# A fused attention and gated-MLP kernel: two moves put on another queue, two sums put ahead of the additions, one transpose group a slot sooner

## The chip, the core and the metric

The kernel runs on one core of one Trainium2 chip. Its time is device microseconds of that core, from start to end of the program. The engines are named as the profile names them: PE (TensorE's matrix products; PEld is its loading of weights), DVE (VectorE), ACT (ScalarE), POOL (GpSimd) and SP (SyncE, which only issues DMAs here). "ACTq" and "SPq" are rows of an engine's sequencer, mostly DMA issues. A line number such as L844 is a line of the kernel before.

## The reference

Eight batches of eight heads attend to keys and values that are averaged over groups of 8 positions; the result, turned into 4608 tokens of 512, goes through two large products with a function between them. All of it is float32.

```python
def _attn_ref(q, k, v):                     # each (8, 8, 576, 64)
    k_p = k.reshape(B, H, 72, 8, D).mean(axis=3)
    v_p = v.reshape(B, H, 72, 8, D).mean(axis=3)
    scores = 1.0 / np.sqrt(D) * np.matmul(q, k_p.transpose(0, 1, 3, 2))
    scores = scores - np.max(scores, axis=-1, keepdims=True)
    attn = np.exp(scores)
    attn = attn / (np.sum(attn, axis=-1, keepdims=True) + 1e-09)
    return np.matmul(attn, v_p)

def _moe_ref(x, w_in, w_out, alpha):        # (4608, 512), (512, 2048), (2048, 512), (2048,)
    h = x @ w_in
    s = np.sin(alpha * h)
    g = h + s * s / (alpha + 1e-09)
    return g @ w_out
```

## The kernel before, in words

**Stages.** A short beginning computes most of batch 0's attention. Then come nine units of 512 tokens each (`hidden`), which compute h, the sine and g and store g to a buffer in DRAM (`g_bridge`). The last stage (`outputs`) reads g back and multiplies by w_out. While unit u computes, it also carries the attention of batch u+1: the functions `exp`, `norm`, `turn`, `move`, `all_values` and so on are called in its slots.

**Slots of a unit.** The product x @ w_in is done by a scheme with seven block products instead of eight. A unit has four groups, J = 0 to 3, of 256 columns of w_in for each half; each group has seven slots, k = 0 to 6, one block product (`product`, L844: four matmuls of 128x128 by 128x256, which the profile shows as eight rows) to a slot. So a unit has 28 slots, and slot 21 is the first of group 3. The products of a group come in the order 1, 5, 6, 2, 7, 3, 4. They accumulate in four PSUM banks, and a group takes four of five banks in turn, so that the first bank of the next group is the one that held `b7` of the group before. Between them ACT copies one bank into the next (`copy`, L820: b6 from b1 in slot k=1, b7 from b6 and p5 from b5 in k=3), takes sines (`sin`, L994) and squares (`square`, L1001), and DVE makes sums (`add`, L819). A product that goes on in a copied bank must wait for the copy.

A group G is not done when its slots are. In k=0 of the next group come its last four sines (`last_sines`), in k=1 its last squares, and in k=2 `finish` adds (L1046, two additions, the first of which reads the old `b7`). In k=3 `store_g` (L1060) sends two DMAs of 512 KB to `g_bridge` from SP. The old group is called Q there. One tile `s` holds the sines of all groups.

**Extras.** `carry(u)` fills a table: slot number to functions. `at(15, A.norm, 2)` puts the call into slot 15. In most slots the extras come ahead of that slot's product; in k=2 they come right after `finish(Q)`, in k=0 after `last_sines(Q)`, in k=1 after the copy and the squares. Every engine runs its instructions in the order in which the program gives them out; nothing else orders them but the waits for data. So a call's slot sets its place in the queues of all engines that it uses.

**Attention of batch 1 in unit 0.** `A` is batch 1 and `A0` batch 0. Its scores are shifted by their maxima into a tile `ex`. `exp(i)` (L366, ACT) works on quarter i in place; switching ACT between sine and exponential shows as ACT_TABLE_LOAD. `norm(i)` sums the exponentials (L372, DVE), inverts the sum (L373, DVE) and multiplies (L374, POOL). `turn(i)` transposes the quarter in blocks of 32x32 on DVE into a tile `tr` (L501 to L511). `move(blocks, queue, halves)` (L514) then copies `tr`, block by block, to the tile `aM`, whose partitions are keys: two DMAs (L521) for each block and half, 32 rows of 736 or 704 columns each, on the given queue, SP if none is given. Half 0 is rows 0 to 63 of `aM`, half 1 rows 64 to 127. Each of the four blocks of `tr` is needed for all 32 rows of a quarter's four turns, so no move can start before the last turn. In slot 26 `all_values` (L600) multiplies `aM` with the averaged values (L610, L623). Its first two matmuls read rows 64 to 127 of all four blocks; the next read rows 0 to 63 also.

**Last weights of batch 0.** The last 64 queries of batch 0 go their own way: `norm_rest` (L450) leaves their weights in the tile `last`, `a_rest` (L487) turns them with five transposes on PE (L491, L492) and copies the result to `last_t` on ACT (L493), and `values_rest` (L587) multiplies it with values (L593, L595) in slot 24. Its four parts write four PSUM banks, the last of them the bank that `finish` has freed.

**What follows on the same queues.** `turn_q` (L215) transposes the queries of batch 2 into the same tile `tr` on DVE (L228 and L233, slots 23 and 24), which has to wait for all moves out of `tr`, and moves them with 16 DMAs on SP (L243, slots 25 and 26). The scores of batch 2 (`two_scores`, L317) read them in slots 3 and 5 of unit 1, after eight and after all of the 16.

**Semaphores of DMAs.** All DMAs of SP and ACT together take eight completion semaphores in turn, in the program's order. A DMA's issue waits for the landing of the last one that had its semaphore, so the 16 moves also wait, each, for one about eight DMAs earlier.

Of the kernel before, what the change touches and what calls it, by code (L numbers as in the profile page):

```python
# [40 lines left out]
class Kernel:  # L41
# [1127 lines left out]
    def carry(self, u):  # L1169

        nc = self.nc
        x = defaultdict(list)
        at = lambda slot, f, *a: x[slot].append(lambda: f(*a))
        last = self.B - 1
        b = u + 1
        if u == 0:
            A0, A = self.att[:2]
            at(1, A0.rest_q)
            at(1, A0.a_head, 1, (5, 6, 2))
            at(1, self.refine)  # L1180
            at(2, A0.values, (2, 3), (2, 1), 1, 1)
            at(2, A0.score, 4)
            at(2, self.sums_of_x, 0, 2)
            at(2, self.sums_of_x, 0, 3)
            at(2, self.load_w_in_part, 2)
            at(2, self.load_w_in_part, 3)
            at(2, self.pairs_q, 1, (0, 1))
            at(3, self.pairs_q, 1, (2, 3, 4))
            at(4, self.combine_w_in, 1, (0, 1, 2, 3), self.nc.gpsimd)
            at(4, A.q_t, 0, self.nc.vector.tensor_copy)  # L1190
            at(4, A.q_t, 1, self.nc.vector.tensor_copy)
            at(4, A.k_t)
            at(7, self.load_v, 1)
            at(7, lambda: self.pool_v())
            for i in range(2):
                at((6, 11)[i], A.two_scores, i)
            at(13, A.two_shifts)
            for i in range(2, 5):
                at((8, 8, 9)[i - 2], A.q_t, i)
            at(9, A0.exp, 4)  # L1200
            for i in range(4):
                at((9, 9, 15, 15)[i], A.exp, i)
                at((10, 10, 16, 16)[i], A.norm, i)
                at((13, 13, 19, 19)[i], A.turn, i)
            at(8, self.combine_w_in, 2, (0, 1, 2, 3), self.nc.gpsimd)
            at(13, A0.norm_rest)
            at(17, self.combine_w_in, 3, (0, 1), self.nc.gpsimd)
            at(17, self.combine_w_in, 3, (2, 3), self.nc.gpsimd)
            at(22, A0.a_rest)
            at(24, lambda: A0.values_rest((5, 6, 7, (self.turn + 1) % 5)))  # L1210
            for r in (32, 96):
                at(3, self.nc.gpsimd.memset, self.aM[r:r + 32, :, 704:736], 0.0)
            at(19, A.move, range(3))
            at(20, A.move, (3,), nc.scalar, (0,))
            at(21, A.move, (3,), nc.scalar, (1,))
            at(26, A.all_values)
            at(9, self.load_q, 2)
            at(23, self.inner_w_in)
            for e in range(2):
                at(12, self.load_k, 2, e)  # L1220
                at(17, lambda e=e: self.pool_k[e]())
            at(27, self.att[2].k_t)
            turn = 23
        else:
            at(0, self.sums_of_x, u, 2)
            at(0, self.sums_of_x, u, 3)
        if 0 < u < last:
            A = self.att[b]
            for i in range(2):
                at((3, 5)[i], A.two_scores, i)  # L1230
            at(6, A.two_shifts)
            for i in range(4):
                at((8, 9, 10, 10)[i], A.exp, i)
                at((9, 10, 11, 12)[i], A.norm, i)
                at((12, 13, 13, 13)[i], A.turn, i)
            at(14, A.move, range(4))
            at(6, self.load_v, b)
            at(12, lambda: self.pool_v())
            for i in range(2):
                if b < last:  # L1240
                    at(12, self.load_k, b + 1, i)
                    at(12, lambda i=i: self.pool_k[i]())
            at(25, A.all_values)
            if b < last:
                at(26, self.att[b + 1].k_t)
            if 2 < u + 2 <= last:
                at(7, self.load_q, u + 2)
            at(2, self.inner_x, u)
            turn = 22
        elif u:  # L1250
            turn = None
        if turn and u + 2 <= last:
            for part in range(4):
                at(((turn, turn + 1) if u == 0 else (23, 24))[part] if part < 2 else turn + part, self.turn_q, u + 2, part)
        if u + 1 < self.NU:
            at(27, self.sums_of_x, u + 1, 0)
            at(27, self.sums_of_x, u + 1, 1)
        return x
# [336 lines left out]
```

## Time and profile before

| what | value |
|---|---|
| time, median of 3 runs | 905.26 us (904.72 to 905.44) |
| the profiled execution's own time | 904.95 us |
| its span, first to last instruction | 903.2 us |
| granted TensorE clock | 1.000 of full speed |
| PE busy | 895.0 us (99%) |
| DVE, ACT, POOL busy | 681.0 (75%), 449.1 (50%), 212.6 us (24%) |
| PE busy from 20 to 57 us | 36.90 of 37.00 us |
| PE busy from 357 to 412 us (a later unit) | 55.00 of 55.00 us |
| last stage, 467 to 903.2 us, PE busy | 431.63 of 436.20 us |

How to read it: times in the timeline are microseconds from the start of the span. A row gives start, duration, engine, line, operation, output tile <- input tiles, shapes, and a count where several are merged. In square brackets stands the idle time of that engine just before the row and, behind the arrow, what ended it. Where a wait is for several things, the last one by the profile is named. In the stretches the columns are PE, PEld, DVE, ACT and POOL busy time with their counts, then the granted clock, the DMA engines' share and GB/s. The chain is the sequence of work that ended last, followed backwards. Matmuls are pipelined, and their ends are modelled; two rows of one slot overlap, so the distance between starts tells more than the durations.

Unit 0 begins at about 20 us. Its slot 20 begins at 65.93, slot 22's product at 70.04, slot 23's at 72.55, and slot 26 (`all_values`) at 79.52. Unit 1 begins at about 87 us.

### The profile page before, as it was taken

Reading aid. Unit: us, or ns where it says so; the run is one execution under the profiler, and the core shown is the slowest. Engines: PE = TensorE matmul, PEld = TensorE weight load, DVE = VectorE, ACT = ScalarE, POOL = GpSimd, SP = SyncE. Lnnn points to the kernel's source line nnn. Section 1 sums busy time; section 2 is a strip of 40 time slices with the busy share of each in tenths; the row PEclk is TensorE's granted clock in tenths of the full one; section 3 lists DMA queues with packets and bytes.
Section 4 is the critical chain, followed back from the end, with each engine's and each line's share of the span. In section 5 each row is a group of like instructions: output and inputs, shape, how many; then the busy total and the mean of one; then the engine's idle time right before and its main releaser. Section 6 shows DMA issues by size and latency. Waiting matters only on the chain.

```text
span 903.2 us, 17920 instructions
## 1 busy us (share of the span) xinstructions
PE 895.0 (99%) x7002; PEld 815.1 (90%) x7002; DVE 681.0 (75%) x1012; ACT 449.1 (50%) x1072; POOL 212.6 (24%) x216
## 2 busy tenths in 40 slices
PE   8999999999999999999999999999999999999998
PEld 5787888888888888888888999999999999999998
DVE  7685766768577685764557799979798888889895
ACT  5686776877768778687976611111111111111111
POOL 5688552824438253430000000000000000000000
PEclk9999999999999999999999999999999999999999
DMA  9965867759577595648217246261618162533401
GB/s 253 255 200 151 219 166 196 194 149 270 145 212 186 174 238 138 180 141 298 93 67 232 98 139 205 53 198 40 224 27 227 37 192 72 171 92 123 141 14 40
DMA packets 128746, 141.12 MB, mean 156 GB/s; under 512 B 46920, under 2 KB 95704, under 8 KB 128664
## 3 DMA queue, kind: packets, MB, share of 16 engines
q1 hardware_dynamic: 125880, 137.88, 53.5%
q10 hardware_dynamic: 2784, 2.11, 0.9%
q8 instruction: 55, 0.90, 0.4%
q14 instruction: 27, 0.22, 0.1%
HBM read 75.37 MB, written 47.19 MB: 136 GB/s over the span
## 4 chain that ended last, share of the span: by engine, by line
PE 95%; DVE 2%; ACT 2%; DMA 1%; POOL 0%; SPq 0%; ACTq 0%; issue 0%; DVEq 0%
PE PS L844 44%; PE PS L1328 41%; PE PS L1024 3%; PE PS L317 2%; PE PS L610 2%; PE PS L623 1%; DMA home<-in_k_dram 1%; DVE x L1283 1%; ACT s L1001 0%; DVE s L1283 0%; DVE r L1283 0%; ACT s L994 0%; PE PS L568 0%; PE PS L289 0%; PE PS L278 0%; PE PS L566 0%
## 5 line engine op out<-in xcount | busy, mean ns | idle before, releaser
L844 PE MATMUL PS<-home,a 128*128 128x256 f32 x1104 | 258.0, 381 | 0.4 <-DVE h L819 0.2
L844 PEld LDWEIGHTS PS<-home,a 128*128 128x128 f32 x1104 | 205.2, 190 | 33.3 <-issue 5.0
L844 PE MATMUL PS<-home,as 128*128 128x256 f32 x768 | 182.9, 382 | 0.5 <-ACT PS L820 0.5
L844 PEld LDWEIGHTS PS<-home,as 128*128 128x128 f32 x768 | 141.6, 190 | 20.6 <-ACT PS L820 1.2
L1378 POOL TENSOR_TENSOR cc<-cc,cb 128x576 f32<-128x576 f32 x1 | 2.0, 1980 | 501.8 <-DVE cb L1283 501.8
L1328 PE MATMUL PS<-s,wb 128*128 128x144 f32 x896 | 119.1, 286 | 0.0
L1328 PEld LDWEIGHTS PS<-s,wb 128*128 128x128 f32 x896 | 113.7, 190 | 0.1
L1001 ACT ACTIVATE s<-s,c 128x256 f32<-128x256 f32 (+1 forms) x228 | 113.5, 564 | 0.0
L819 DVE TENSOR_TENSOR h<-PS,p 128x512 f32<-128x512 f32 x72 | 49.2, 683 | 62.0 <-PE PS L844 36.9
L131 POOL TENSOR_TENSOR kvin<-kvin 96x768 f32<-96x768 f32 (+3 forms) x42 | 72.7, 1731 | 71.7 <-DMA kvin<-in_v_dram 69.3
L1456 ACT COPY PS<-PS 128x144 f32<-128x144 f32 x56 | 14.7, 263 | 144.8 <-PE PS L1328 138.1
L994 ACT ACTIVATE s<-h,al 128x256 f32<-128x256 f32 x144 | 65.6, 509 | 38.3 <-DVE h L819 38.1
L1328 PE MATMUL PS<-r,wb 128*128 128x144 f32 x512 | 73.3, 286 | 0.3 <-DVE r L1283 0.3
L1328 PE MATMUL PS<-s,a 128*128 128x144 f32 x512 | 73.2, 286 | 0.0
L994 ACT ACTIVATE s<-PS,al 128x256 f32<-128x256 f32 x144 | 60.2, 470 | 20.2 <-PE PS L844 19.2
L1046 DVE TENSOR_TENSOR h<-PS,s 128x512 f32<-128x512 f32 x36 | 24.7, 685 | 58.6 <-ACT s L1001 58.6
L1328 PEld LDWEIGHTS PS<-r,wb 128*128 128x128 f32 x512 | 67.1, 190 | 0.5 <-DVE r L1283 0.5
L1328 PEld LDWEIGHTS PS<-s,a 128*128 128x128 f32 x512 | 67.0, 190 | 0.0
L820 ACT COPY PS<-PS 128x512 f32<-128x512 f32 x72 | 41.5, 576 | 34.9 <-PE PS L844 30.1
L1476 ACT COPY PS<-PS 128x144 f32<-128x144 f32 x56 | 14.7, 263 | 88.1 <-PE PS L1328 88.1
L1046 DVE TENSOR_TENSOR h<-h,s 128x1024 f32<-128x1024 f32 x36 | 57.1, 1586 | 0.9 <-ACT s L1001 0.9
L1328 PE MATMUL PS<-x,wb 128*128 128x144 f32 x384 | 54.9, 286 | 0.0
(216 smaller groups left out, 1409.6 us busy)
## 6 DMA issues: line engine op xcount, KB each, us to landing
g_bridge<-h SPq DMA_DIRECT2D x72, 512.0 KB
r<-g_bridge SPq DMA_DIRECT2D x31, 1152.0 KB
out_dram<-o SPq DMA_DIRECT2D x122, 72.0 KB
kvin<-in_k_dram SPq DMA_DIRECT2D x14, 576.0 KB
q<-in_q_dram SPq DMA_DIRECT2D x7, 1024.0 KB
kvin<-in_v_dram SPq DMA_DIRECT2D x14, 512.0 KB
aM<-tr SPq DMA_DIRECT2D x54, 92.0 KB
aM<-tr SPq DMA_DIRECT2D x54, 88.0 KB
```

Source lines behind the costliest of these rows:

```text
L131: self.nc.gpsimd.tensor_tensor(out=t[..., 0:w] if w > D else out, in0=t[..., 0:w], in1=t[..., w:2 * w], op=OP.add)
L317: nc.tensor.matmul(ps[e][r0 + r:r0 + r + q.shape[-1], h, :], q[s], kb[s, hp, :], start=True, stop=True)
L610: nc.tensor.matmul(o[r:r + 64], w, x, start=start and i < 2, stop=False, skip_group_check=True)
L819: add = lambda o, x, y: nc.vector.tensor_tensor(out=o, in0=x, in1=y, op=OP.add)
L820: copy = lambda o, x: nc.scalar.copy(out=o, in_=x)
L844: nc.tensor.matmul(ps[:, jj, :], self.A[p][:, kk, f * P:(f + 1) * P], x[:, kk, :], start=(start and n == 0), stop=(kk == 1), skip_group_ch ...
L994: self.nc.scalar.activation(out=G.s[:, i, jj, j, :], in_=src[:, jj], func=AF.Sin, scale=self.al[:, f:f + 1])
L1001: self.nc.scalar.activation(out=x, in_=x, func=AF.Square, scale=self.c[:, f:f + 1])
L1024: nc.tensor.matmul(o, W[m][:, G.J - J0], X[m], start=start and n == 0, stop=True, skip_group_check=True)
L1046: add = lambda o, x, y: self.nc.vector.tensor_tensor(out=o, in0=x, in1=y, op=OP.add)
L1328: nc.tensor.matmul(out, W[:, J // 2, J % 2, :], A[:, J, :], start=(start and J == 0), stop=(J == self.NJ - 1), skip_group_check=True)
L1456: nc.scalar.copy(out=x1[:, 0, :], in_=x0[:, 1, :])
```

## The change

Four calls in the table of unit 0 get another slot or another queue. `norm(2)` and `norm(3)` are called in slot 15, after `exp(2)` and `exp(3)`, instead of slot 16, where `finish` came ahead of them: on DVE their two sums and two reciprocals (L372, L373) stood after the two additions L1046 and before the next addition, an L819; now they stand ahead of all three. `a_rest` is called in slot 21 instead of 22: its five transposes come ahead of slot 21's product on PE, and its copy L493 stands on ACT after the last four sines, ahead of the copy L820 that it used to follow with the squares. Of the four moves of block 3, the two of half 0 go to SP's queue, behind the twelve moves of blocks 0 to 2, instead of ACT's. The two of half 1 stay on ACT, where they stand, as before, after the four sines; L493 is now between. No computation and no DMA is added or removed. The completion semaphores of the 16 moves are dealt out anew among the same eight; from the next store on they are the same as before.

```diff
             for i in range(4):
                 at((9, 9, 15, 15)[i], A.exp, i)
-                at((10, 10, 16, 16)[i], A.norm, i)
+                at((10, 10, 15, 15)[i], A.norm, i)
                 at((13, 13, 19, 19)[i], A.turn, i)
...
-            at(22, A0.a_rest)
+            at(21, A0.a_rest)
             at(24, lambda: A0.values_rest((5, 6, 7, (self.turn + 1) % 5)))
...
             at(19, A.move, range(3))
-            at(20, A.move, (3,), nc.scalar, (0,))
+            at(20, A.move, (3,), nc.sync, (0,))
             at(21, A.move, (3,), nc.scalar, (1,))
             at(26, A.all_values)
```

## The prediction

> **What bounds the kernel now.** I read the page's busy times first, then the stretches, then the chain of waits, then the timeline of the stretch that the change touches.
>
> ```profile
> PE 895.0 (99%) x7002; PEld 815.1 (90%) x7002; DVE 681.0 (75%) x1012; ACT 449.1 (50%) x1072; POOL 212.6 (24%) x216
> 57.00:82.00 25.00, 23.86 (x168) 18.64 (x170) 16.23 (x29) 17.11 (x36) 22.28 (x21) 1.00 0.48 147
> 82.00:137.00 55.00, 55.00 (x448) 46.27 (x449) 38.40 (x62) 40.84 (x95) 28.18 (x31) 1.00 0.67 177
> ```
>
> TensorE bounds all: the units after the first have no hole in PE (55.00 of 55.00 us), but the end of the first unit has 1.14 us of holes in 25 us. Only there can the change win anything, and it can't win much.
>
> ```profile
> 67.05 0.71 DVE tr L501
> ...
> 68.54 0.54 ACTq L521
> 69.12 0.86 ACTq L521
> 70.02 0.51 ACT s L994
> ...
> 71.84 0.57 ACT PS L820
> 72.41 2.04 ACT s L1001 x4
> 74.45 0.32 ACT last_t L493
> ```
>
> The chain leaves PE at 56.8 and comes back at 74.81 through POOL, DVE and ACT. Two links are DMA issues (L521) in ScalarE's queue. The same stretch in the timeline:
>
> ```profile
> 61.29 0.63 DVE L1046 TENSOR_TENSOR h<-PS,s 128x512 f32<-128x512 f32 x1
> 63.06 0.75 DVE L372 TENSOR_REDUCE sm<-ex 128x8 f32<-128x584 f32 x1
> 64.19 2.83 POOL L374 TENSOR_TENSOR ex<-ex,sm 128x576 f32<-128x576 f32 x2 [0.33 <-ACT s L994]
> 67.05 0.71 DVE L501 STREAM_TRANSPOSE tr<-ex 128x512 f32<-128x512 f32 x1 [0.36 <-POOL ex L374]
> 68.45 0.65 DVE L819 TENSOR_TENSOR h<-PS,p 128x512 f32<-128x512 f32 x1
> 68.46 7.62 SPq L521 DMA_DIRECT2D aM<-tr  x12
> 70.13 0.52 ACTq L521 DMA_DIRECT2D aM<-tr  x1
> 72.55 1.97 PE L844 MATMUL PS<-home,as 128*128 128x256 f32 x8 [0.52 <-ACT PS L820]
> 74.48 0.69 DVE L1046 TENSOR_TENSOR h<-PS,s 128x512 f32<-128x512 f32 x1 [4.79 <-ACT s L1001]
> 74.81 0.75 PE L593 MATMUL PS<-last_t,vm 64*64 64x64 f32 x16 [0.29 <-ACT last_t L493]
> 77.66 2.37 DVE L228 STREAM_TRANSPOSE tr<-q 128x1024 f32<-128x1024 f32 x2 [1.02 <-DMA aM<-tr]
> 79.52 0.65 PE L610 MATMUL PS<-aM,vm 64*64 64x512 f32 x6
> ```
>
> PE waits at 72.55 for the copy L820 and at 74.81 for L493. DVE sits idle at 67.05 for POOL's multiplication; at 77.66 the last aM moves land.
>
> **Sums ahead of the additions.** On DVE the two sums and reciprocals take 61.29's place. Their stretch (63.06 to the next addition at 65.19) moves 1.77 us forward; the first sum is ready at about 62.27, the second at 63.47. POOL is busy until 63.86 (L463: 63.57 + 0.29), so its two multiplications start at 63.86 instead of 64.19 and end 0.33 earlier, at 66.70. DVE's 0.36 idle before 67.05 shrinks to 0.03, so the turns end at about 68.20 and L819 (68.45) runs 68.12 to 68.77. The additions L1046 end 2.1 us later, at 65.25. Behind them waits the store to g_bridge (L1060, issued at 63.16): it goes at 65.3, on a queue that stands idle until the moves. The PSUM bank that the first frees is wanted at 67.8 by the next group's first product (its slot begins one PE slot, 1.83, after 65.93), 3.8 us after it is free. Next to POOL work the second addition took 1.29 at 61.85 and 1.55 at 75.09, so it may grow by 0.26, and delay L819 at 65.19, for which product 4 (65.93, 0.21 idle <- DVE) waits. Ends 0 and 0.26; I take 0, by the row at 61.85 that also had POOL at work beside it.
>
> **Two moves off ScalarE's queue.** The sines at 70.02 wait for L819 (69.10) and stand behind two DMA issues, 0.54 and 0.86. Without these they start 0.03 after L819 (as 65.88 to 65.91): at 68.80, 1.22 earlier. Four take 1.63 (70.02 to 71.65): 70.43. The two issues that stay come after them and L493. If the sequencer runs ahead, as at 70.13, when one issue went out while three sines had yet to start, they lie beside the sines and cost nothing. If they stand in line they cost 1.04 to 1.40 (twice 0.52, or 0.54 + 0.86) and the whole gain of the copy goes. I take nothing, since the row at 70.13 is this very pair.
>
> In the Trainium skill, Perfetto Trace Analysis, "DVE / Act Engine Instruction", the sequencer is free once an instruction stands in the wait queue; by that rule they cost nothing too, and the trace agrees at 70.13.
>
> **Last weights one slot sooner.** The five transposes (0.45 of PE) trade places with product 1; no PE time is added. Their input was ready at 63.86. The copy L493 costs ScalarE 0.30 (74.36 to 74.66) ahead of L820 instead of after the squares. L820 then starts at 70.43 - 0.09 overlap + 0.30 = 70.65, not 71.84: 1.19 earlier. `last_t` is there at 70.75, and the wait at 74.81 has no cause left.
>
> **PE from there.** Product 5 starts at 70.04 as before. A slot takes 1.83 (3.65 for 16 in the chain), so product 6 can start at 71.87; L820 ends at 71.22. That saves 0.68 of 72.55. The last values follow at 73.70 instead of 74.81: 1.11. Their last four rows write the bank that L1046 (74.48 to 75.17) reads; that hangs on L820 by 3.33 us and comes at 73.98. So PE is 1.11 to 1.19 early, say 1.15, and reaches L610 at 78.37.
>
> **The moves on SyncE's queue** are what is late next. It now issues 14 from 68.13. Twelve starts from 68.46 to 75.50 give 0.64 each, so the 14th starts at 76.45. The last one's landing is in two rows:
>
> ```profile
> 75.50 0.59 SPq L521 DMA_DIRECT2D aM<-tr  x1
> ```
>
> 75.50 to 77.66 (L228's release) is 2.16, so the 14th lands at 78.61. The first two matmuls of all_values read rows 64 to 127 alone and can start at 78.37; the next read the block of the 14th. PE waits some 0.24, and the gain is 1.15 - 0.24 = 0.91. Bounds of the landing: with one issue less in the way 0.64 earlier, no wait (1.15); with one of 1.69, as the queue's longest in this stretch (the fourth q move), 1.05 later (a loss of 0.1).
>
> The Trainium skill (DMA: Bandwidth & Descriptors, "Issuing engines are not separate DMA queues") says that an issue is usually small beside its transfer. By that the two would cost nothing and the gain would be 1.15; here 12 issues fill 7.62 us, so I follow the row.
>
> L228 too waits for the 14th: 78.61, 0.95 later. Behind it on DVE stand L233 and the L819 of 80.55, wanted by product 4 after 85.21: 4 us of room. The q moves behind L233 (80.65) go 0.95 later. Their first eight are issued by 87.22, last landing by some 88.9, now 89.9, for scores that PE starts at 92.28, now 91.4; the other eight end issuing at 92.30, now 93.25, and land at about 94.8, for 97.19, now 96.3. Both have over a microsecond. The next store (76.67) stands behind the two moves until 77.1: nobody waits for it.
>
> **Sum.** 904.95 (the profiled execution; span 903.2 and 1.75 around it) - 0.91 = 904.04. The median of the runs, 905.26, lies 0.31 above it: 904.35.
>
> **The rivals.**
> *In line.* ScalarE issues its two DMAs only when its sines are done. L820 then starts at 71.5 to 71.9, PE keeps most of the wait at 72.55, and the one at 74.81 can go only in part: a gain of 0 to 0.4, 905.1. Against it: 70.13.
> *SyncE too late (slower).* The place is L610. It decides once the 14th move lands after 79.5, 0.9 later than reckoned; each issue of 1.69 costs 1.05. For it: that row, and the delayed stores, which share the engines until about 69.7. One such issue gives 905.4; two or three, or a part of a move that lags on one DMA engine, 906.4 to 907.5.
> *Later rhythm.* Every later unit has its own length, 55.06 to 55.25 from one L623 group to the next. A PE that is 0.9 early against the same queues may gain or lose up to 0.2 in each of six units: 1.2 either way, 903.2 or 905.5; with a wait at a q move more. Against it: PE shows no hole there.
>
> **How the numbers follow.** Forecast 0.54, in line 0.13, SyncE too late 0.17, later rhythm 0.16. Two runs of this kernel can tell a difference from about 0.2%, here 1.8 us. The forecast and in line lie within it. SyncE too late is over it for 0.09, the rhythm for 0.11 below and 0.05 above. So faster 0.11, same 0.75, slower 0.14. The likeliest range is 903.8 to 905.0; to hold eight in ten it goes from 903.3 (largest gain 1.2, some rhythm, scatter 0.4) to 906.0 (one long issue and scatter).
>
> **What would show it.** Right: sines near 68.8, ScalarE's issues beside them, L820 near 70.65, no hole at 72.55 and 74.81, 14 SyncE issues 0.64 apart, a hole of a quarter microsecond within the first rows of L610, L228 near 78.6. Wrong: L820 after 71.5 (in line), L610 after 79.5 (SyncE), holes in PE after 82 (rhythm); or POOL's multiplication still at 64.19, which would take the first 0.33 away.

## The result and the profile after

The changed kernel takes 907.89 us (median of 9 runs, 906.04 to 910.14) beside 905.43 (9 runs, 904.61 to 906.03): a ratio of 1.003, 95% interval 1.0018 to 1.0042. It is slower, by 2.46 us (0.3%) in the median. The profiled execution is one of the longer runs: 909.65, 4.70 over the profiled 904.95 of before.

Busy times on the page and two stretches of the kernel after (start and end, length, then busy time and count of PE, PEld, DVE, ACT and POOL, the granted clock, the DMA share and GB/s):

```profile
PE 898.1 (99%) x7002; PEld 817.6 (90%) x7002; DVE 678.9 (75%) x1012; ACT 448.8 (49%) x1072; POOL 211.9 (23%) x216
57.00:82.00 25.00, 21.69 (x107) 17.28 (x107) 14.94 (x26) 15.64 (x31) 22.65 (x21) 0.86 0.38 108
69.00:75.00 6.00, 5.83 (x16) 4.30 (x17) 3.45 (x11) 2.97 (x7) 5.86 (x5) 0.50 0.74 239
82.00:137.00 55.00, 55.00 (x443) 46.58 (x442) 37.70 (x63) 39.14 (x91) 28.18 (x31) 1.00 0.70 192
```

All of the loss but 0.24 us lies in the stretch that the change touches. PE's holes there grew from 1.14 to 3.31 us, and from 69 to 75 PE was granted half its clock. From 82 to 137 PE has no hole and the full clock, as before.

The chain of waits in the kernel after (start, length, what) leaves PE at 64.25 and comes back at 69.17, through DVE alone:

```profile
64.25 0.03 DVEq L819
64.29 4.22 DVE h L1046 x2
68.51 0.61 DVE h L819
...
69.17 3.78 PE PS L844 x8
```

The DMA issues and the copy that stood in the chain before are gone from it. The timeline of the kernel after shows why DVE is there:

```profile
62.08 1.18 POOL L459 TENSOR_TENSOR last<-ex,sm 64x256 f32<-64x256 f32 x2 [1.88 <-DVE sm L455]
63.48 2.73 POOL L374 TENSOR_TENSOR ex<-ex,sm 128x576 f32<-128x576 f32 x2
63.98 0.63 DVE L1046 TENSOR_TENSOR h<-PS,s 128x512 f32<-128x512 f32 x1
64.52 3.99 DVE L1046 TENSOR_TENSOR h<-h,s 128x1024 f32<-128x1024 f32 x1
66.17 1.25 POOL L685 TENSOR_TENSOR as<-a,a 128x512 f32<-128x512 f32 x1
67.50 2.13 POOL L685 TENSOR_TENSOR as<-as,a 128x512 f32<-128x512 f32 x1
68.44 0.68 DVE L819 TENSOR_TENSOR h<-PS,p 128x512 f32<-128x512 f32 x1
69.17 3.78 PE L844 MATMUL PS<-home,a 128*128 128x256 f32 x8 [3.20 <-DVE h L819]
...
84.26 0.65 PE L610 MATMUL PS<-aM,vm 64*64 64x512 f32 x6
```

In the kernel before, the addition, the sum behind it and product 4 were these rows:

```profile
61.85 1.29 DVE L1046 TENSOR_TENSOR h<-h,s 128x1024 f32<-128x1024 f32 x1
65.19 0.69 DVE L819 TENSOR_TENSOR h<-PS,p 128x512 f32<-128x512 f32 x1
65.93 3.72 PE L844 MATMUL PS<-home,a 128*128 128x256 f32 x16 [0.21 <-DVE h L819]
```

The second addition took 3.99 us where it took 1.29 before. It stands beside POOL rows that follow one another without a break from 63.48 on. They leave off at 67.42 (66.17 + 1.25) for 0.08. The addition ended at 68.51, 1.09 later, which is about what it needs in all; and the L685 that starts at 67.50 took 2.13 instead of 1.25. So by these rows each engine stood still while the other worked. The L819 behind the addition came at 68.44 instead of 65.19, and PE waited 3.20 us for it. The eight matmuls that follow took 3.78; eight rows of a slot took 1.99 before (at 70.04).

The account at `all_values`, in these two executions: L610 starts 4.74 later (84.26 to 79.52). The whole stretch had begun 0.24 later, slot 20 another 3.00 later (69.17 - 65.93 - 0.24), and from slot 20 to L610 it took 15.09 instead of 13.59. Of the 3.00 the addition's growth is 2.70. Most of the rest came ahead of the sums: POOL's L374 of quarters 0 and 1, which DVE's turns wait for, started 0.41 later against PE (57.95 to 57.30, less the 0.24). The waits for the copy and for L493 did go; the lower clock took more than that back. Experiment 6 splits the 1.50 between 15.09 and 13.59 into a gain of 1.31 and a loss of 2.81.

The mean granted clock of the nine runs is 0.999 in the two shortest (906.04 and 906.5), 0.996 in 909.18 and 909.65, and 0.997 or 0.998 in the other five, the longest (910.14) among them. Half the clock for 3.5 us, as in experiment 2, makes some 0.002 of the mean (an estimate: 3.5 x 0.5 / 908). So the fall was of different length from run to run. In the two shortest there may have been none, since 31 of the 66 runs of the kernel before beside the experiments show 0.999 too.

### The profile page after: what moved, and what is told of

Same layout as the page of the kernel before. It is cut to its first block, busy times and chain, and to the rows that moved or that the text cites. A ratio compares the mean times of both kernels' runs of the same rounds, so it can differ in the third digit from the quotient of the medians.

```text
span 907.9 us, 17919 instructions
## 1 busy us (share of the span) xinstructions
PE 898.1 (99%) x7002; PEld 817.6 (90%) x7002; DVE 678.9 (75%) x1012; ACT 448.8 (49%) x1072; POOL 211.9 (23%) x216
## 4 chain that ended last, share of the span: by engine, by line
PE 97%; DVE 2%; ACT 0%; issue 0%; DVEq 0%
PE PS L844 45%; PE PS L1328 41%; PE PS L1024 3%; PE PS L317 2%; PE PS L610 2%; PE PS L623 1%; DVE x L1283 1%; DVE h L1046 0%; PE PS L1092 0%; DVE s L1283 0%; PE PS L422 0%; DVE r L1283 0%; PE PS L400 0%; PE PS L568 0%; PE PS L289 0%; PE PS L278 0%
## 5 line engine op out<-in xcount | busy, mean ns | idle before, releaser
L844 PE MATMUL PS<-home,a 128*128 128x256 f32 x1104 | 260.9, 384 | 3.4 <-DVE h L819 3.2
L819 DVE TENSOR_TENSOR h<-PS,p 128x512 f32<-128x512 f32 x72 | 49.2, 683 | 64.3 <-PE PS L844 38.5
L131 POOL TENSOR_TENSOR kvin<-kvin 96x768 f32<-96x768 f32 (+3 forms) x42 | 72.4, 1723 | 71.4 <-DMA kvin<-in_v_dram 69.4
L1046 DVE TENSOR_TENSOR h<-PS,s 128x512 f32<-128x512 f32 x36 | 24.7, 685 | 60.5 <-ACT s L1001 60.5
L820 ACT COPY PS<-PS 128x512 f32<-128x512 f32 x72 | 41.5, 576 | 38.3 <-PE PS L844 31.3
L1046 DVE TENSOR_TENSOR h<-h,s 128x1024 f32<-128x1024 f32 x36 | 54.5, 1513 | 0.9 <-ACT s L1001 0.9
```

The source lines that it names most:

```text
L131: self.nc.gpsimd.tensor_tensor(out=t[..., 0:w] if w > D else out, in0=t[..., 0:w], in1=t[..., w:2 * w], op=OP.add)
L819: add = lambda o, x, y: nc.vector.tensor_tensor(out=o, in0=x, in1=y, op=OP.add)
L820: copy = lambda o, x: nc.scalar.copy(out=o, in_=x)
L844: nc.tensor.matmul(ps[:, jj, :], self.A[p][:, kk, f * P:(f + 1) * P], x[:, kk, :], start=(start and n == 0), stop=(kk == 1), skip_group_ch ...
L1046: add = lambda o, x, y: self.nc.vector.tensor_tensor(out=o, in0=x, in1=y, op=OP.add)
```

## The experiments

Two explanations stood against each other. *Port*: DVE and POOL can't read the same memory at the same time when DVE's instruction has both inputs in SBUF, and the sums, put ahead, move the addition beside a run of POOL instructions. *Queue*: the two moves and the earlier L493 made the end of the unit late. Ratios are to the kernel before on the same chip: 905.5 us (903.97 to 907.21) beside experiments 1 to 4, 905.49 (903.61 to 908.13) beside 5 to 8.

**1. All but the sums.** The kernel after, with `norm(2)` and `norm(3)` back in slot 16:

```diff
-                at((10, 10, 15, 15)[i], A.norm, i)
+                at((10, 10, 16, 16)[i], A.norm, i)
```

> Theory (port): the loss comes from the sums put ahead of the additions, because the second addition L1046 (two SBUF inputs) then falls beside POOL's multiplications L374 and can't run until POOL pauses. With the sums back in slot 16 that addition takes its 1.3 us again, PE has no hole at slot 20 and the clock stays at 1.00: some 904.8 us, 0.6 below before (PE 0.9 early, 14th move landing at about 78.9 takes 0.3 of it). Rival (queues): the two moves on SyncE's queue or the order of the last weights cost the time: it stays at 907 or more.

904.56 us (903.92 to 905.7), ratio 0.9988 (0.9979 to 0.9997). The timeline of this kernel:

```profile
62.01 1.29 DVE L1046 TENSOR_TENSOR h<-h,s 128x1024 f32<-128x1024 f32 x1
66.10 1.99 PE L844 MATMUL PS<-home,a 128*128 128x256 f32 x8 [0.63 <-DVE h L819]
```

Without the sums ahead the addition takes 1.29 again, PE waits 0.63 and not 3.20, and the two other parts together bring 0.94. (The 0.63 is above the 0.21 of before because POOL and DVE were again some 0.4 late against PE.)

**2. The sums alone.** The kernel before, with

```diff
-                at((10, 10, 16, 16)[i], A.norm, i)
+                at((10, 10, 15, 15)[i], A.norm, i)
```

> Theory (port): this part alone brings the whole loss: L1046's second addition takes 3 us or more beside L374, L819 comes late, PE has a hole of some 3 us at slot 20, and where the hole is long enough the granted clock falls to 0.5 for some microseconds: 907 to 911 us with a wide scatter. Rival (queues): without the other two parts it is no slower than before, at most 0.3 us faster.

907.6 us (906.1 to 911.5), ratio 1.0027 (1.0015 to 1.004). Its timeline:

```profile
62.87 2.73 POOL L374 TENSOR_TENSOR ex<-ex,sm 128x576 f32<-128x576 f32 x2
63.91 3.99 DVE L1046 TENSOR_TENSOR h<-h,s 128x1024 f32<-128x1024 f32 x1
68.56 5.41 PE L844 MATMUL PS<-home,a 128*128 128x256 f32 x16 [3.20 <-DVE h L819]
```

The 3.99 and the 3.20 are here with neither of the other parts. The moves and L493 are cleared: the loss belongs to the sums.

**3. The two moves alone.** The kernel before, with

```diff
-            at(20, A.move, (3,), nc.scalar, (0,))
+            at(20, A.move, (3,), nc.sync, (0,))
```

> Theory (port): nothing of the loss is here. The sines start 0.9 earlier (69.1), L820 at about 70.7, and the 14th move lands at 78.9 against 79.5: 904.8 us, 0.6 below before. Rival (queues): the loss is here: 907 or more.

904.3 us (902.88 to 905.17), ratio 0.9986 (0.9977 to 0.9994). Its timeline:

```profile
69.02 0.59 ACTq L521 DMA_DIRECT2D aM<-tr  x1
69.01 0.51 ACT L994 ACTIVATE s<-h,al 128x256 f32<-128x256 f32 x1 [2.31 <-DVE h L819]
70.58 0.57 ACT L820 COPY PS<-PS 128x512 f32<-128x512 f32 x1
78.26 0.65 PE L610 MATMUL PS<-aM,vm 64*64 64x512 f32 x6
78.78 2.37 DVE L228 STREAM_TRANSPOSE tr<-q 128x1024 f32<-128x1024 f32 x2 [2.90 <-DMA aM<-tr]
78.80 0.20 PEld L610 LDWEIGHTS PS<-aM,vm 64*64 64x64 f32 x4 [0.21 <-DMA aM<-tr]
```

The issue lies beside the sines, the copy comes 1.26 earlier, L610 is 1.26 earlier, and a weight load within it waits 0.21 for a move: nearly all the steps that the prediction drew, brought about by this one part.

**4. The last weights alone.** The kernel before, with

```diff
-            at(22, A0.a_rest)
+            at(21, A0.a_rest)
```

> Theory (port): nothing of the loss is here. The copy L493 stands ahead of L820 and delays it by up to 0.3, the wait at 74.81 goes: between 905.0 and 905.7, no difference that can be told. Rival (queues, order): slower by over 1 us.

905.81 us (903.43 to 907.47), ratio 1.0001 (0.9993 to 1.001): no difference. Its timeline:

```profile
73.39 1.97 PE L844 MATMUL PS<-home,as 128*128 128x256 f32 x8 [0.57 <-ACT PS L820]
76.07 0.33 PE L593 MATMUL PS<-last_t,vm 64*64 64x64 f32 x4 [0.34 <-DVE h L1046]
```

The wait for L493 goes. But L493, a copy on ACT, now stands ahead of the copy L820, which keeps its wait (0.57), and the last four rows of `values_rest` wait for the addition that reads their bank (0.34). Beside the moves it may even cost a little: in the profiled executions, from slot 20's product to L610 experiment 3, without it, needs 12.45 us (65.81 to 78.26), experiment 1, with it, 12.75 (66.10 to 78.85), where the same four rows wait 0.26. The medians (904.3 and 904.56) are too close to show it.

**5. The addition on POOL.** The kernel after, with that one addition given to the other engine, where it stands in line with the multiplications:

```diff
-            add(Q.g[:, :, :, 1], Q.g[:, :, :, 1], Q.s[:, :, :, 1])
+            (self.nc.gpsimd if (Q.u, Q.J) == (0, 1) else self.nc.vector).tensor_tensor(
+                out=Q.g[:, :, :, 1], in0=Q.g[:, :, :, 1], in1=Q.s[:, :, :, 1], op=OP.add)
```

> The changed kernel with the one addition of group 1 that took 3.99 us (two SBUF inputs) done by POOL, behind its two multiplications. Theory (port): DVE has nothing left there that needs what POOL holds, so L819 runs at about 64.7 and PE has no hole before slot 20; the price is paid elsewhere: the store waits for POOL's addition (some 2.6 us behind 66.2), the 14 moves stand behind the store, the last lands at 80 or later and L610 waits for it: about 906 to 907 us, clock 1.00. Rival (order of the instructions on DVE or PE, not the port): the hole before slot 20 stays at 3 us and the time at 908 or more.

906.37 us (904.74 to 909.38), ratio 1.0016 (1.0004 to 1.0027). Its timeline:

```profile
65.40 1.89 PE L844 MATMUL PS<-home,a 128*128 128x256 f32 x8
65.42 2.35 POOL L1050 TENSOR_TENSOR h<-h,s 128x1024 f32<-128x1024 f32 x1
68.80 10.36 SPq L521 DMA_DIRECT2D aM<-tr  x14
79.55 0.65 PE L610 MATMUL PS<-aM,vm 64*64 64x512 f32 x6 [1.32 <-DMA aM<-tr]
80.76 0.20 PEld L610 LDWEIGHTS PS<-aM,vm 64*64 64x64 f32 x4 [0.78 <-DMA aM<-tr]
```

The hole before slot 20 is gone, so the addition was its cause. The time isn't won: the addition (2.35 on POOL) ends at 67.77, and the store that needs it goes at 67.80; the 14 moves behind it on SP's queue take 10.36 instead of the 8.84 of experiment 7 (that the store's own transfer slows them is likely, but not shown), and PE waits twice for them at L610, 1.32 and 0.78. That is the prediction's rival "SyncE too late", in a kernel that makes its condition true.

**6. The hole filled.** The kernel after, with 14 matmuls in slot 20 ahead of product 4, whose result nobody reads (`full` is a bf16 tile of the kernel, bank 5 is free then):

```diff
+    def fill(self, n):
+        for _ in range(n):
+            self.nc.tensor.matmul(self.psum([P, 4, P], 5), self.full[:],
+                self.full[:].unsqueeze(1).to_broadcast([P, 4, P]), start=True, stop=True)
...
-            at(21, A0.a_rest)
+            at(21, A0.a_rest); at(20, self.fill, 14)
```

> The changed kernel with 14 idle matmuls (the start-up's filler, 0.22 us each, whose result nobody reads) put into the hole before slot 20. Theory (clock): the hole is a loss of its own, and the fall of the granted clock to 0.5 after it another: with the filler the clock stays at 1.00, product 4 starts where it did, and the rows after it are 0.22 and not 0.43 us apart: some 906.5 to 907.5 us, with less scatter, none over 908.5. Rival (the hole alone): median and scatter as in the changed kernel, 907.9 (906.0 to 910.1).

906.63 us (905.9 to 907.88), ratio 1.0019 (1.001 to 1.0028). A stretch and, below it, the timeline of this kernel:

```profile
57.00:82.00 25.00, 24.89 (x159) 18.89 (x159) 16.34 (x27) 16.64 (x35) 22.65 (x23) 1.00 0.42 127
```

```profile
63.63 4.00 DVE L1046 TENSOR_TENSOR h<-h,s 128x1024 f32<-128x1024 f32 x1
65.17 3.19 PE L66 MATMUL PS<-full 128*128 128x512 bf16 x14
68.28 1.99 PE L844 MATMUL PS<-home,a 128*128 128x256 f32 x8
```

The addition is as long as in the kernel after (4.00), yet the clock stays at 1.00 and the eight matmuls take 1.99 instead of 3.78. So the hole, not the slow addition, let the clock fall. L610 starts at 80.56 here, 12.28 after slot 20's product; in the kernel after it was 15.09. The clock cost 2.81 between these two executions and 1.26 in the medians (907.89 to 906.63). With it much of the scatter is gone (2 us between the extremes here, 4.1 there), and all eleven runs show 0.999 or 1.000.

**7. A pause on POOL.** The kernel after, with an addition of 128x1 on POOL between the two multiplications, into a tile that nobody reads:

```diff
+    def pause(self):
+        y, x = self.sm.tile([P, 1], F32, name="pause")[:], self.ex[:, 2, 0, 0:1]
+        self.nc.gpsimd.tensor_tensor(out=y, in0=x, in1=x, op=OP.add)
...
-                at((10, 10, 15, 15)[i], A.norm, i)
+                at((10, 10, 15, 15)[i], A.norm, i); i != 2 or at(15, self.pause)
```

> The changed kernel with one POOL addition of 128x1, whose result nobody reads, between the two multiplications; it reads the first one's result and so has to wait for it, which makes POOL pause. Theory (the port is held until POOL pauses): the second addition L1046 gets through at that pause: 1.3 to 2.4 us instead of 3.99, the second multiplication starts 1.0 to 1.3 later, the hole before slot 20 is under 1 us, the clock stays at 1.00: some 905.0 to 906.0 us. Rival (the two engines share the port element by element, and the addition is merely slowed): the pause of 0.1 us changes nothing, 3.9 us, 907.9.

904.38 us (902.93 to 906.06), ratio 0.9992 (0.9983 to 1.0001). Its timeline:

```profile
62.84 1.14 POOL L374 TENSOR_TENSOR ex<-ex,sm 128x576 f32<-128x576 f32 x1
63.88 1.21 DVE L1046 TENSOR_TENSOR h<-h,s 128x1024 f32<-128x1024 f32 x1
64.06 1.08 POOL L66 TENSOR_TENSOR pause<-ex 128x1 f32<-128x1 f32 x1
65.75 1.99 PE L844 MATMUL PS<-home,a 128*128 128x256 f32 x8 [0.18 <-DVE h L819]
70.68 0.60 ACT L820 COPY PS<-PS 128x512 f32<-128x512 f32 x1
78.40 0.65 PE L610 MATMUL PS<-aM,vm 64*64 64x512 f32 x6
78.61 2.37 DVE L228 STREAM_TRANSPOSE tr<-q 128x1024 f32<-128x1024 f32 x2 [2.92 <-DMA aM<-tr]
```

DVE gets in at once and takes 1.21. Now POOL stands still: one element in each partition takes it 1.08, up to the end of DVE's addition. Two engines that share the memory element by element would have left the addition at some 3.9. More work on POOL, and 3.5 us less time than the kernel after. This is the test that the queue explanation can't pass, since no move and no copy was touched.

**8. The moves, and the first turns later.** The kernel before with experiment 3's edit, and with the turns of the first two quarters called in slot 17 instead of 13. On DVE they then stand behind the additions L1046, which come earlier instead of later:

```diff
-                at((13, 13, 19, 19)[i], A.turn, i)
+                at((17, 17, 19, 19)[i], A.turn, i)
```

> The kernel before with the two moves on SyncE's queue, the sums left behind the additions, and instead the turns of quarters 0 and 1 put behind them all (slot 17 instead of 13), so that additions and sums come forward together. Theory (port): the second addition now starts at about 59.2, beside the last of the multiplications of quarters 0 and 1, which ends at 59.6 and after which POOL waits: at most 0.4 us longer. Sums ready by about 63, the multiplications of quarters 2 and 3 end by some 66, and the 0.36 us that DVE waits for them at 67 goes: 0.2 to 0.4 better than the move alone, some 904.0 us. Rival: the turns moved back push L819 past 65.2 and open the hole before slot 20 wider: 904.6 or more.

903.07 us (902.57 to 904.75), ratio 0.9977 (0.9968 to 0.9986): the shortest time of all the kernels here. A stretch and the timeline of this kernel:

```profile
57.00:82.00 25.00, 24.89 (x177) 19.67 (x176) 15.55 (x29) 17.79 (x39) 23.99 (x25) 1.00 0.49 149
```

```profile
59.03 2.16 POOL L459 TENSOR_TENSOR last<-ex,sm 64x256 f32<-64x256 f32 x2
59.32 1.41 DVE L1046 TENSOR_TENSOR h<-h,s 128x1024 f32<-128x1024 f32 x1
...
77.72 0.65 PE L610 MATMUL PS<-aM,vm 64*64 64x512 f32 x6
```

The addition meets only the two short L459 and takes 1.41, and PE works 24.89 of 25.00 us. L610 is 1.80 earlier than before, and the profiled execution 1.88 shorter (903.07 to 904.95). That is more than expected: against experiment 3 the moves begin at 67.14 instead of 68.34, and the waits of 0.29 before slot 20 and of 0.21 within L610 are gone.

## Why the prediction was wrong

**The step that failed** is this one: "Next to POOL work the second addition took 1.29 at 61.85 and 1.55 at 75.09, so it may grow by 0.26 ... Ends 0 and 0.26; I take 0". It grew by 2.70. The two rows chosen were the mild ones, and already the same hold, cut short: the first of the two L459 beside 61.85 ended at 62.06, 0.21 later, and the addition 1.08 after that. The same line has a much longer row in the kernel before, which the trace shows when the forms of the line are kept apart (counts, then minimum, median and maximum duration in ns):

```profile
L1046 DVE TENSOR_TENSOR h<-PS,s x36: 631/692/693, 44.2 to 519.1; 128x512 f32<-128x512 f32 x36
L1046 DVE TENSOR_TENSOR h<-h,s x36: 1175/1308/3260, 44.8 to 519.7; 128x1024 f32<-128x1024 f32 x36
```

The form with both inputs in SBUF goes from 1175 to 3260, the form with one input in PSUM never leaves 631 to 693. The 3260 is the row at 44.79, and the timeline of the kernel before says what stood beside it:

```profile
44.62 4.58 POOL L131 TENSOR_TENSOR kvin<-kvin 128x1024 f32<-128x1024 f32 x2 [5.71 <-DMA kvin<-in_v_dram]
44.79 3.26 DVE L1046 TENSOR_TENSOR h<-h,s 128x1024 f32<-128x1024 f32 x1
61.45 2.16 POOL L459 TENSOR_TENSOR last<-ex,sm 64x256 f32<-64x256 f32 x2 [1.88 <-DVE sm L455]
```

An upper end of 3.26 - 1.18 = 2.08 stood there to be taken, instead of 0.26; it is more than three quarters of the 2.70. It isn't all of it. The first L131 of the pair at 44.62 took 2.35 and ended at 46.97, and the addition ended 1.08 after it. So do all 20 rows of this form in the kernel before that have POOL at work beside them: each ended 1.08 after a POOL instruction did, and none waited for more than one. (The 16 others took 1.18 to 1.23.) In the kernel after, the addition waited for three POOL instructions, the end of one and two whole ones, and then took 1.09; no row of before shows that. In the Trainium skill, SBUF — State Buffer, "SBUF: two separate sides", a DVE operation with two SBUF inputs and a POOL operation that reads SBUF exclude each other: the first to start has the shared ports for its whole instruction. The rows agree that the other is shut out; but here the addition, waiting since 64.52, was also passed by the L685 at 66.17, which started later.

**What followed from it** had no rival: none of the prediction's rivals had the L819 late. That L819 was named (the 0.26 was said to "delay L819 at 65.19, for which product 4 ... waits"), so with 2.08 at the upper end the sum would have reached 906.4. And a hole in PE was priced at its length alone. The clock's fall behind it doubled that in the profiled execution (3.00 and 2.81).

**POOL's start** came out too pessimistic, from the same cause. The prediction kept POOL busy until 63.86. The pair L459 at 61.45 took 2.16 only because the addition at 61.85 held it up; with the addition gone from there it took 1.18, and the multiplications began at 63.48 in the kernel after (62.84 in experiment 7), not 63.86. The store at "65.3" went at 68.54.

**With the hold taken away the rest holds.** Experiment 7 is the changed kernel without it: L820 at 70.68 (70.65 predicted), L610 at 78.40 (78.37), L228 at 78.61 (78.61), time 904.38 (904.35). That L610 agrees to 0.03 is partly luck: slot 20 began 0.18 earlier than in the kernel before (65.75 to 65.93), and PE gave 0.15 of it back at 74.11, where the last four rows of `values_rest` waited for L1046, a wait that the prediction had not reckoned with. The 14 issues are 0.63 apart (8.84 in all; 0.64 predicted). The quarter microsecond at L610 is missing there but shows in experiment 3 (0.21). The issue beside the sines is right in experiments 1, 3 and 7, so "in line" did not occur; neither did the "later rhythm", since the 4.74 at L610 is the 4.70 of the whole time. "SyncE too late" did not occur in the changed kernel, and did in experiment 5.

**One term was sized right and put to the wrong part.** The 1.1 that PE gains was credited to the moves and the earlier `a_rest` together. The moves alone give it (experiment 3), `a_rest` alone gives nothing (experiment 4).

**What stays open**: when DVE is let in. In the kernel after and in experiments 2 and 6 it waited until POOL's first break, past two whole POOL instructions; at 61.85 of the kernel before and at 59.32 of experiment 8 it got in between the two L459, which show no break. The rows hold a hint. Where it got in, the addition started 0.17 and 0.28 ahead of POOL's next instruction (62.02 and 59.60); in the three slow cases it started only 0.06 or 0.07 ahead (64.52 to 64.58, 63.91 to 63.98, 63.63 to 63.69). That could be why it missed the first turn, but not why it missed the second, at L685. No run changes that distance alone.

## What to carry to other kernels

Before moving a DVE operation with two SBUF inputs, look at what POOL does at its new place, and take its worst row in the whole trace as the upper end, by form, not the row nearest in time; where POOL runs several instructions without a break, even that row can be too small (2.08 against 2.70 here). Where TensorE waits for what stands behind such an operation, put it where POOL pauses; here one tiny POOL instruction that had to wait made the pause. Price a hole in TensorE of some 3 us at up to twice its length, and look at the granted clock behind it.

## What the runs showed of the hardware

- A 128x1024 addition of float32 with both inputs in SBUF takes 1.18 to 1.23 us where POOL is idle. Beside a working POOL it ended 1.08 after a POOL instruction did, in 20 of 20 rows of the kernel before, and took 1.28 to 3.26. It took 3.99 beside POOL instructions without a break (two kernels, and 4.00 in a third). POOL is held in the same way: 2.13 instead of 1.27, 1.08 for a 128x1 operation. A DVE operation with one input in PSUM (0.63 at 63.98) or with one input in all (L372, 0.70 at 61.93) was not held by such work.
- After a hole of 3.20 us the clock was granted at 0.50. In the profiled execution of the kernel after, 0.86 over 25 us means 7 us at half clock; in that of experiment 2, with a hole of the same length, 0.93 means 3.5 us. The fall has no fixed place after the hole's start: 0.54 from 68.50 to 69.00 in the kernel after puts it at 68.5, 0.6 before PE came back; 0.68 from 69.00 to 71.50 in experiment 2 puts it at 69.9, 1.3 after PE came back at 68.56. In the Trainium skill, TensorE: Matmul & The Clock Gate, "What's actually happening", the clock is halved after an idle window of about 3.4 us, and comes back after a busy one; the runs agree in the halving and in steps of about that length, with a hole that is a little shorter.
- Fourteen matmuls whose result is thrown away held the clock at 1.00 through the same gap.
